# Two small reorderings in a fused attention and expert kernel: where the norm scales of every second group are made, and which of two PSUM copies goes first

## The chip, the cores and the metric

The kernel runs on one core of one Trainium2 chip. The metric is the device time of one execution in microseconds (us), as the median of several runs. The profiled execution is one more run with its own time.

## The reference: attention with normalised queries and keys, then eight experts with a limited capacity

Shapes: q, k, v are 8 batches x 12 heads x 448 rows x 64; the experts are 8, each with two weight matrices (768x1024 and 1024x768) and room for 80 rows.

```
rmsnorm(x, g) = x / sqrt(mean(x*x, -1) + 1e-6) * g
scores = rmsnorm(q) @ rmsnorm(k).T / 8
attn   = softmax(scores) @ v                # becomes x: 3584 rows of 768
logits = x @ w_gate ; expert = argmax(logits) ; gate = max softmax prob
each expert keeps its 80 rows of highest gate
out[rows] = gate * (relu(x[rows] @ w1[e]) @ w2[e])   # all other rows 0
```

## The kernel before: a hand-written order of slots

The 96 heads are handled four at a time, as 24 groups g (three per batch). A group has seven rounds. A round is one `score` (two 448-wide score products on TensorE, `ps`, L359, and their exponential on ScalarE, `at`, L362), one `presum` (VectorE adds `at` into the running sum `sm`, L392 and L394) and one `av` (TensorE, `po`, L376). The kernel is written out as a list of slots. Slot s issues the scores of rounds 2s and 2s+1 and the sums and products of the two rounds before. Group g begins in slot b0 = 7g//2. Every engine works through its own instructions in the order in which the slots issue them. Within a slot the order is: the slot's loads (`begins`), the two scores, `pre`, the presums, `mid`, the products `av`, then the lists `ahead` and `end`.

Preparation of a group is spread over the slots before it:

- `load_qk` in slot b0-11 (SyncE's queue; q and k have four buffers in all, so a load waits for `normalise` of the group two before).
- `square` (ScalarE, L270) and `squares` (VectorE row sums `ms`, L278) in slots b0-7 and b0-6.
- `rstd` in slot b0-5: two ScalarE instructions (Ln L289, Exp L290), then three short ones on VectorE (L291 to L293). `normalise` for q (a=0) follows in the same slot, for k (a=1) one slot later; both are VectorE, L306.
- `transp` for k and then for q in slot b0-2: 28 transposes on TensorE (`tp`, L314) and two ScalarE copies out of PSUM, `qkT` (L349 for k, L347 for q). These two are called the pair below. For odd g, slot b0-5 of group g is slot b0-2 of group g-1, so the pair of group g-1 stands in the `end` list of the slot whose `mid` list holds `rstd(g)`.

Around it run, per batch: `zl` (48 TensorE products for gate logits and softmax sums, L411, which need `sm` and `us` of the batch's three groups; slot b0+5 of its last group), `gate1` (ScalarE copies L421 and L423, a VectorE add L424), `gate1v`, `gate2` and others, and `merge`, which keeps a list of the best rows per expert. `merge` makes the row of gate weights (`row`: eight transposes, ScalarE copy L543, needed by the comparisons `vbeat`, L550 and L553). `xout` turns a group's result into rows (16 transposes into `xp`, ScalarE copy `xb`, L654) and stores it to HBM. For the first group of each batch but the first, `xout` falls into the same `end` list as `row` of the batch before.

PSUM buffers: the tag `sc` has two, shared in turn by every `ps`, by the k half of the pair, by `zl`, and by `merge`'s scratch, `row` included. The tag `tp` has one: the q half of the pair, `xp`, the turned gate sums. `at` has six buffers in SBUF.

In the code the lists are run so, at the end of each slot:

```
for f, a in ahead.pop(s, []) + end.pop(s, []):
    f(*a)
```

After the last group the experts run: gather of rows, two products per expert, scaling and a scatter of the output.

Of the kernel before, what the change touches and what calls it, by code (L numbers as in the profile page):

```python
# [21 lines left out]
def kernel(  # L22
# [31 lines left out]
    NQ = H // 4  # L54
# [178 lines left out]
    with av_stack:  # L233
# [3 lines left out]
        st = [dict() for _ in range(NG)]  # L237
# [74 lines left out]
        def turned(o, w, p):  # L312
            one = ident if w.dtype == F32 else identb
            nc.tensor.transpose(o, w, one[p, p], tile_position=(p.start, 0))  # L314
# [36 lines left out]
        def score(r):  # L351
            g, x = divmod(r, RD)
            T0, T1 = st[g]["T0"], st[g]["T1"]
            ps = scps.tile([128, 2, 512], F32, tag="sc", name="ps")
            at = apool.tile([128, 2, S], F32, tag="at", name="at")
            for u in range(2):
                for hh in range(2):
                    d = slice(hh * D, (hh + 1) * D)
                    nc.tensor.matmul(ps[u * 64:u * 64 + 64, hh, :S],  # L359
                                     T1[d, u, x * 64:(x + 1) * 64], T0[d, u, :],  # L360
                                     start=True, stop=True)
            nc.scalar.activation(at[:], ps[:, :, :S], AF.Exp)  # L362
            st[g]["at%d" % x] = at

        def av(r):
            g, x = divmod(r, RD)
            vt, at = st[g]["v"], st[g]["at%d" % x]
            if x == 0:
                po = pops.tile([128, 2, 512], F32, tag="po", name="po")
                other = po if g < NG - 1 else tpps.tile([128, 2, 512], F32, tag="tp", name="po")  # L370
                st[g]["po"] = (po, other)
            po = st[g]["po"]
            for u in range(2):
                p = slice(u * 64, u * 64 + 64)
                for hh in range(2):
                    nc.tensor.matmul(po[u][hh * D:(hh + 1) * D, u, :S],  # L376
                                     vt[p, hh * NX + x, :], at[p, hh, :],
                                     start=(x == 0), stop=(x == RD - 1))
            if x == RD - 1:
                st[g]["us"] = upool.tile([128, 2, S], F32, tag="us", name="us")  # L380

                n = 2 if g < NG - 1 else 1
                nc.scalar.copy(st[g]["us"][:, :n], po[0][:, :n, :S])  # L383
                if n < 2:
                    nc.vector.tensor_copy(st[g]["us"][:, n:], po[1][:, n:, :S])
# [253 lines left out]
        def xout(g):  # L639

            b, i = divmod(g, NQ)
            pool, tag = ((tpps, "tp"), (scps, "sc"), (pops, "po"))[
                max(0, g - NG + 3) or int(i == NQ - 1)]
            xp = pool.tile([128, 2, 512], F32, tag=tag, name="xp")
            us = st[g]["us"]
            for j in range(NJ + 1):
                for u in range(2):
                    c = slice((2 * j + u) * 64, (2 * j + u) * 64 + 64)
                    for hh in range(2):
                        p = slice(64 * hh, 64 * hh + 64)  # L650
                        t = min(j * 128, S - 128)
                        turned(xp[:, hh, c], us[p, u, t:t + 128], p)
            xb = prep.tile([128, NJ + 1, 256], F32, tag="xb", name="xb")
            nc.scalar.copy(xb[:].rearrange("p j (u hh d) -> p hh (j u) d", u=2, hh=2),  # L654
                           xp[:].rearrange("p hh (k d) -> p hh k d", d=D))
            st[g]["xb"] = xb
            if g < NG - 2:
                xstore(g)

        def xstore(g):  # L660
            b, i = divmod(g, NQ)
            xb = st[g]["xb"]
            rows = xr_dram[b * S:(b + 1) * S, i * 256:(i + 1) * 256].rearrange(
                "(p x) d -> p x d", x=NX)
            for t in range(2):
                nc.sync.dma_start(out=rows[:, t:SM // 64:2], in_=xb[64 * t:64 * t + 64, :NJ])
            nc.sync.dma_start(out=rows[:, NX - 1], in_=xb[64:, NJ])
# [25 lines left out]
        begins, pre, mid, end = {}, {}, {}, {}  # L693

        def at_slot(where, s, f, *a):
            where.setdefault(s, []).append((f, a))

        ahead = {}

        def first(s, f, *a):  # L700
            ahead.setdefault(s, []).append((f, a))
# [15 lines left out]
        for g in range(NG):  # L717
            b0 = g * RD // 2
            at_slot(begins, max(b0 - 11, -10), load_qk, g)
            at_slot(begins, b0 - 4, load_v, g)  # L720
            if g:
                for a in range(2):
                    at_slot(mid, b0 - 7 + a if g > 1 else -1, square, g, a)
                    at_slot(end, b0 - 7 + a if g > 1 else -1, squares, g, a)
                at_slot(mid, b0 - 5 if g > 1 else 0, rstd, g)
                for a in range(2):
                    at_slot(mid, b0 - 5 + a if g > 1 else 0, normalise, g, a)
            if g:
                for a in (0, 1) if g == 1 else (1, 0):
                    at_slot(end, b0 - 2 + (a if g == 1 else 0), transp, g, a)  # L730
            if g < NG - 2:
                i = g % NQ
                x0 = ((NQ * (g // NQ) - 1) * RD // 2 + 10 + 3 * i) if g >= NQ else 6 + 3 * i
                at_slot(end, b0 + 6 if i == NQ - 1 else x0, xout, g)
        for b in range(B):
            b0 = (NQ * b + NQ - 1) * RD // 2
            if b == B - 1:
                at_slot(end, b0 + 3, zl, b, range(NQ - 1))
                at_slot(end, b0 + 4, xout, NG - 2)
                at_slot(end, b0 + 4, zl, b, range(NQ - 1, NQ))  # L740
                at_slot(end, b0 + 4, gate1, b)
                at_slot(end, b0 + 4, xout, NG - 1)
                at_slot(end, b0 + 5, gate1t, b)
                at_slot(mid, b0 + 6, gate1v, b)
                continue
            first(b0 + 5, zl, b, range(NQ))
            first(b0 + 5, gate1, b)
            at_slot(end, b0 + 6, gate1t, b)
            at_slot(mid, b0 + 7, gate1v, b)
            at_slot(mid, b0 + 7, gate2, b)  # L750
            at_slot(mid, b0 + 8, gate2i, b)
            at_slot(end, b0 + 8, gate2x, b)
            at_slot(pre, b0 + 9, gate2b, b)
            at_slot(pre, b0 + 9, gate2p, b)
            for t, fs in enumerate(merge(b)):


                if b == B - 2 and t > 3:
                    at_slot(end, b0 + 12 + t, fs[0])
                    continue  # L760
                s = 15 + b % 2 if b < B - 2 else 13
                (first if t else lambda *a: at_slot(end, *a))(
                    b0 + (10, 10, 12, s, 18 + b % 2, 20 + b % 2)[t], fs[0])
                for n, f in enumerate(fs[1:]):
                    at_slot(end, b0 + (10, 11, 12, s)[t], f)
# [11 lines left out]
        for e in range(E):  # L777
            for i in range(2):
                s = 9 + 23 * (2 * e + i) // 5
# [11 lines left out]
        for s in range(-10, NS + 6):  # L791
            for f, a in begins.pop(s, []):
                f(*a)
            S2 = [r for r in (2 * s, 2 * s + 1) if 0 <= r < NG * RD]
            A2 = [r for r in (2 * s - 2, 2 * s - 1) if 0 <= r < NG * RD]

            for r in A2:
                if r % RD == RD - 1 and r < A2[-1]:
                    av(r)
            for r in S2:  # L800
                score(r)
            for f, a in pre.pop(s, []):
                f(*a)
            for r in A2:
                presum(r)
            for f, a in mid.pop(s, []):
                f(*a)
            for r in A2:
                if r % RD < RD - 1 or r == A2[-1]:
                    av(r)  # L810
            for f, a in ahead.pop(s, []) + end.pop(s, []):
                f(*a)
        assert not ahead
        assert not begins and not pre and not mid and not end
    mpool = ctx.enter_context(tc.tile_pool(name="moe_sb", bufs=2))

# [39 lines left out]
    ahead = tpool.tile([128, NT, CAP], BF16, tag="ahead", name="ahead")  # L856
# [187 lines left out]
```

## Time and profile before

| | |
|---|---|
| median of 3 runs | 422.82 us (422.19 to 422.96) |
| profiled execution | 423.0 us, its span 421.3 us |
| TensorE (PE) busy | 399.1 us, 95% |
| VectorE (DVE) busy | 357.5 us, 85% |
| ScalarE (ACT) busy | 314.9 us, 75% |
| GpSimd (POOL) busy | 73.5 us, 17% |
| granted TensorE clock, mean | 0.998 |

The span is from the first to the last instruction; 1.7 us of the execution's time lies around it. The ends of matmuls in the profile are modelled. "Idle before" in a row is the time in which the engine had nothing running before that instruction, with what ended it. A row of the timeline merges neighbouring instructions of a kind, with their count.

### The profile page before, as it was taken

What the parts mean: (1) busy time and instruction counts of PE and PEld (TensorE: products, weight loads), DVE (VectorE), ACT (ScalarE), POOL (GpSimd) and SP (SyncE); (2) the same over time, 40 slices, a digit from 0 to 9 for tenths busy, and PEclk for the clock granted to TensorE, in tenths of its full rate; (3) what the DMA queues carried; (4) which work ended last, traced back from release to release, by engine and by line L of the source; (5) the groups of instructions that cost most, each with busy time, mean ns of one, the idle gap of its engine ahead of it and who ended that gap; (6) DMA issues with size and microseconds to landing.
All of it is one profiled execution on the core that took longest, in us unless ns stands there. A gap on an engine that the chain in (4) does not pass through costs nothing.

```text
span 421.3 us, 12543 instructions
## 1 busy us (share of the span) xinstructions
PE 399.1 (95%) x5289; PEld 194.9 (46%) x5289; DVE 357.5 (85%) x641; ACT 314.9 (75%) x479; POOL 73.5 (17%) x118
## 2 busy tenths in 40 slices
PE   6799999999989999999899999999999999889993
PEld 6334444444444445444444444443444443448882
DVE  5699889998999999989999999989999779735550
ACT  5898979997889799979798799878997784202120
POOL 2000001301040205100420024001500050134321
PEclk9999999999999999999999999999999999999999
DMA  7355599999959999999799969999799298869981
GB/s 261 123 149 140 152 224 317 282 254 268 287 166 206 326 230 274 242 237 320 234 236 233 338 172 195 232 286 338 170 237 312 59 358 211 270 213 339 342 301 47
DMA packets 75983, 100.91 MB, mean 240 GB/s; under 512 B 8344, under 2 KB 65176, under 8 KB 75928
## 3 DMA queue, kind: packets, MB, share of 16 engines
q1 hardware_dynamic: 59856, 70.53, 52.2%
q0 software_dynamic: 15776, 29.13, 36.1%
q8 instruction: 41, 0.67, 0.6%
q10 hardware_dynamic: 296, 0.46, 0.4%
q14 instruction: 14, 0.11, 0.1%
HBM read 101.11 MB, written 39.89 MB: 335 GB/s over the span
## 4 chain that ended last, share of the span: by engine, by line
PE 69%; DMA 12%; DVE 10%; ACT 5%; issue 2%; SPq 0%; POOLq 0%; DVEq 0%; ACTq 0%
PE ps L359 26%; PE po L376 26%; DMA w_sb<-wb_scratch 5%; PE zl L411 4%; DMA qk<-in_k_dram 4%; PE tp L314 3%; PE xp L314 3%; DVE ms L278 2%; DVE sm L394 2%; DMA xr_scratch<-xb 2%; PE py L992 1%; DVE qn L306 1%; PE ph L973 1%; ACT qkT L349 1%; DMA xg<-xr_scratch,idxG 1%
## 5 line engine op out<-in xcount | busy, mean ns | idle before, releaser
L359 PE MATMUL ps<-qkT 64*64 64x448 f32 x1344 | 147.9, 548 | 7.6 <-ACT qkT L349 3.2
L362 ACT ACTIVATE at<-ps 128x896 f32<-128x896 f32 x168 | 146.4, 931 | 2.5 <-PE ps L359 1.6
L376 PE MATMUL po<-at,vt 64*64 64x448 f32 x1344 | 142.4, 537 | 0.1
L394 DVE TENSOR_TENSOR sm<-sm,at 128x896 f32<-128x896 f32 x120 | 132.0, 1100 | 2.9
L376 PEld LDWEIGHTS po<-at,vt 64*64 64x64 f32 x1344 | 50.0, 133 | 74.9 <-issue 64.3
L359 PEld LDWEIGHTS ps<-qkT 64*64 64x64 f32 x1344 | 43.1, 132 | 73.2 <-issue 23.5
L278 DVE TENSOR_REDUCE ms<-sq 128x14 f32<-128x896 f32 (+1 forms) x50 | 51.9, 1044 | 6.6 <-ACT sq L270 6.4
L306 DVE TENSOR_TENSOR qn<-qk,rs 128x896 f32<-128x896 f32 (+1 forms) x50 | 52.5, 1052 | 1.9
L270 ACT ACTIVATE sq<-qk 128x896 f32<-128x896 f32 (+1 forms) x50 | 46.3, 929 | 2.8 <-DMA qk<-in_q_dram 2.8
L518 POOL CAST pt<-gw 128x4 bf16<-128x4 f32 x8 | 6.9, 866 | 201.9 <-DVE gw L491 201.9
L977 ACT ACTIVATE h_sb<-ph 128x320 bf16<-128x320 f32 x16 | 7.0, 437 | 39.8 <-PE ph L973 39.8
L654 ACT COPY xb<-xp 128x1024 f32<-128x1024 f32 x24 | 24.3, 1011 | 9.7 <-PE xp L314 9.6
L314 PEld LDWEIGHTS tp<-ident,qn 64*128 64x128 f32 x672 | 23.4, 139 | 11.1 <-issue 5.3
L314 PE MATMUL tp<-ident,qn 64*128 64x64 f32 x672 | 26.9, 226 | 0.0
L383 ACT COPY us<-po 128x896 f32<-128x896 f32 (+1 forms) x24 | 21.4, 893 | 6.2 <-PE po L376 6.2
L392 DVE TENSOR_TENSOR sm<-at 128x896 f32<-128x896 f32 x24 | 25.9, 1081 | 0.0
L347 ACT ACTIVATE qkT<-tp,gqk 128x896 f32<-128x896 f32 x23 | 23.5, 1023 | 0.0
L349 ACT COPY qkT<-tp 128x896 f32<-128x896 f32 x24 | 21.9, 913 | 1.3 <-PE tp L314 1.2
L992 PE MATMUL py<-w_sb,h_sb 128*80 128x384 bf16 (+1 forms) x136 | 22.2, 317 | 0.6 <-DMA w_sb<-wb_scratch 0.6
L996 DVE TENSOR_SCALAR yo<-py,gwT 80x384 f32<-80x384 f32 (+1 forms) x16 | 9.5, 600 | 14.9 <-PE py L992 14.7
L411 PE MATMUL zl<-us,wgs 64*32 64x448 f32 x192 | 21.0, 540 | 0.0
L411 PE MATMUL zl<-sm,zsel 64*32 64x448 f32 x192 | 20.5, 540 | 0.0
(170 smaller groups left out, 412.0 us busy)
## 6 DMA issues: line engine op xcount, KB each, us to landing
wb_scratch<-in_moe_w_dram POOLq DMA_DIRECT2D x20, 768.0 KB, 14.9
w_sb<-wb_scratch SPq DMA_DIRECT2D x9, 1536.0 KB, 8.1
vt<-in_v_dram SPq DMA_DIRECT2D x24, 448.0 KB, 6.3
out_dram<-zeros SPq DMA_DIRECT2D x28, 384.0 KB, 8.2
qk<-in_q_dram SPq DMA_DIRECT2D x23, 448.0 KB, 5.0
qk<-in_k_dram SPq DMA_DIRECT2D x23, 448.0 KB, 6.6
xr_scratch<-xb SPq DMA_DIRECT2D x48, 192.0 KB, 10.2
w_sb<-in_moe_w_dram POOLq DMA_DIRECT2D x6, 1536.0 KB, 15.7
```

The source lines that it names most:

```text
L270: nc.scalar.activation(st[g]["sq%d" % a][:, lo:hi], st[g]["qk"][a][:, lo:hi], AF.Square)
L278: nc.vector.reduce_sum(out=st[g]["ms"][:, a, lo:hi], in_=st[g]["sq%d" % a][:, lo:hi], axis=AX.X)
L306: nc.vector.tensor_mul(qn[:].rearrange("p (x hh) d -> p hh x d", hh=2)[:, h0:h1], qk[:, lo:hi].rearrange("p (hh x) d -> p hh x d", x=NX), ...
L314: nc.tensor.transpose(o, w, one[p, p], tile_position=(p.start, 0))
L349: nc.scalar.copy(T[:], tp[:, :, :S])
L359: nc.tensor.matmul(ps[u * 64:u * 64 + 64, hh, :S], T1[d, u, x * 64:(x + 1) * 64], T0[d, u, :], start=True, stop=True)
L362: nc.scalar.activation(at[:], ps[:, :, :S], AF.Exp)
L376: nc.tensor.matmul(po[u][hh * D:(hh + 1) * D, u, :S], vt[p, hh * NX + x, :], at[p, hh, :], start=(x == 0), stop=(x == RD - 1))
L392: nc.vector.tensor_add(s["sm"][:], s["at0"][:], s["at1"][:])
L394: nc.vector.tensor_add(s["sm"][:], s["sm"][:], s["at%d" % x][:])
L411: nc.tensor.matmul(t[32 * c:32 * c + 32, r, :S], w, x, start=(i == 0), stop=(i == NQ - 1))
L992: nc.tensor.matmul(py[:, :c1 - c0], h_sb[:, fc, :], chunk(e, 1, fc)[:, c0:c1], start=(fc == 0), stop=(fc == FC - 1))
```

## The change: what is reordered

Two things are put elsewhere in the order; no instruction is added or taken away.

1. For odd g above 1 (g = 3, 5, ..., 23: 11 groups), `rstd(g)` and `normalise(g, 0)` go from the `mid` list of slot b0-5 to its `end` list, where they stand behind the pair of group g-1. `normalise(g, 1)` stays in `mid` of the next slot. What stands in `ahead` of that slot now comes before them too, and what the batch loop puts into `end` comes behind them, as before.
2. `xout` is split: for the first group of each batch but the first (g = 3, 6, ..., 21: 7 groups) its copy and store (`xcopy`) go into a new list `after`, run behind `end`. The copy of `row` then stands ahead of the copy of `xb`.

```diff
+            st[g]["xp"] = xp
+            if not (g % NQ == 0 and g >= NQ):
+                xcopy(g)
+
+        def xcopy(g):
+            xp = st[g]["xp"]
             xb = prep.tile([128, NJ + 1, 256], F32, tag="xb", name="xb")
             nc.scalar.copy(xb[:].rearrange("p j (u hh d) -> p hh (j u) d", u=2, hh=2),
                            xp[:].rearrange("p hh (k d) -> p hh k d", d=D))
...
-        ahead = {}
+        ahead, after = {}, {}
...
-                at_slot(mid, b0 - 5 if g > 1 else 0, rstd, g)
+                late = g > 1 and g % 2
+                at_slot(end if late else mid, b0 - 5 if g > 1 else 0, rstd, g)
                 for a in range(2):
-                    at_slot(mid, b0 - 5 + a if g > 1 else 0, normalise, g, a)
+                    at_slot(end if late and not a else mid, b0 - 5 + a if g > 1 else 0,
+                            normalise, g, a)
...
                 at_slot(end, b0 + 6 if i == NQ - 1 else x0, xout, g)
+                if i == 0 and g >= NQ:
+                    at_slot(after, x0, xcopy, g)
...
-            for f, a in ahead.pop(s, []) + end.pop(s, []):
+            for f, a in ahead.pop(s, []) + end.pop(s, []) + after.pop(s, []):
                 f(*a)
```

## Rows read from the trace of the kernel before

**Rows 1.** Busy time by stage: one period of two batches, 206.67 to 294.11 us

```profile
206.67:294.11 87.44, 85.90 (x1164) 38.02 (x1164) 83.04 (x139) 76.37 (x117) 15.26 (x24) 1.00 0.97 245
```

**Rows 2.** Timeline of PE: start, duration, what, count, idle before and its releaser

```profile
204.45 0.98 PE L359 MATMUL ps<-qkT 64*64 64x448 f32 x8
...
206.67 0.98 PE L359 MATMUL ps<-qkT 64*64 64x448 f32 x8 [1.23 <-ACT qkT L349]
...
210.21 0.98 PE L359 MATMUL ps<-qkT 64*64 64x448 f32 x8
211.63 0.98 PE L359 MATMUL ps<-qkT 64*64 64x448 f32 x8 [0.44 <-ACT row L543]
...
292.43 0.98 PE L359 MATMUL ps<-qkT 64*64 64x448 f32 x8
294.11 0.98 PE L359 MATMUL ps<-qkT 64*64 64x448 f32 x8 [0.69 <-ACT qkT L349]
```

**Rows 3.** Chain of waits: start, duration, what (a pair of scores without a wait)

```profile
214.12 1.50 PE ps L359 x16
```

**Rows 4.** Timeline of ACT around the stalls at 206.67 and 211.63

```profile
205.25 0.32 ACT L289 ACTIVATE rs<-ms,eps 128x28 f32<-128x28 f32 x1 [1.05 <-DVE ms L278]
205.59 0.23 ACT L290 ACTIVATE rs<-rs 128x28 f32<-128x28 f32 x1
205.73 0.89 ACT L349 COPY qkT<-tp 128x896 f32<-128x896 f32 x1
...
210.08 1.01 ACT L654 COPY xb<-xp 128x1024 f32<-128x1024 f32 x1
210.99 0.59 ACT L543 COPY row<-mp 128x512 f32<-128x512 f32 x1
```

**Rows 5.** Timeline of ACT, first instruction behind the pair in group 17's slot

```profile
237.08 1.75 ACT L362 ACTIVATE at<-ps 128x896 f32<-128x896 f32 x2
```

**Rows 6.** Timeline of DVE from group 17's norm scales to the next batch's gate sums

```profile
233.73 0.18 DVE L291 SCALAR_TENSOR_TENSOR nw<-rs 128x28 f32<-128x28 f32 x1
...
235.53 0.63 DVE L424 TENSOR_TENSOR zsb<-zsb,zo 128x448 f32<-128x448 f32 x1
236.07 0.19 DVE L603 TENSOR_TENSOR rnk<-back,eq 128x32 f32<-128x32 f32 x1
...
249.23 0.19 DVE L489 TENSOR_REDUCE lsum<-lex 128x4 f32<-128x32 f32 x1 [0.20 <-ACT lex L481]
...
270.58 2.28 DVE L394 TENSOR_TENSOR sm<-sm,at 128x896 f32<-128x896 f32 x2
...
276.56 0.63 DVE L424 TENSOR_TENSOR zsb<-zsb,zo 128x448 f32<-128x448 f32 x1 [1.70 <-ACT zo L423]
```

**Rows 7.** Timeline of PE: a gate product of the batch's third group

```profile
274.51 0.54 PE L411 MATMUL zl<-sm,zsel 64*32 64x448 f32 x2
```

**Rows 8.** Timelines of DVE and ACT around group 16's norm scales

```profile
219.71 1.08 DVE L278 TENSOR_REDUCE ms<-sq 128x14 f32<-128x896 f32 x1
...
221.17 0.38 ACT L289 ACTIVATE rs<-ms,eps 128x28 f32<-128x28 f32 x1
...
222.12 1.01 ACT L654 COPY xb<-xp 128x1024 f32<-128x1024 f32 x1 [0.31 <-PE xp L314]
...
226.07 0.91 ACT L383 COPY us<-po 128x896 f32<-128x896 f32 x1 [0.45 <-PE po L376]
```

**Rows 9.** Timeline of DVE in the first period and after the last norm scales

```profile
72.51 1.09 DVE L278 TENSOR_REDUCE ms<-sq 128x14 f32<-128x896 f32 x1 [0.56 <-ACT sq L270]
74.40 0.19 DVE L489 TENSOR_REDUCE lsum<-lex 128x4 f32<-128x32 f32 x1 [0.81 <-ACT lex L481]
...
336.67 0.19 DVE L489 TENSOR_REDUCE lsum<-lex 128x4 f32<-128x32 f32 x1 [2.19 <-ACT lex L481]
```

**Rows 10.** Timeline of ACT: squares that wait for a load of q

```profile
196.54 0.95 ACT L270 ACTIVATE sq<-qk 128x896 f32<-128x896 f32 x1 [0.29 <-DMA qk<-in_q_dram]
...
284.67 0.96 ACT L270 ACTIVATE sq<-qk 128x896 f32<-128x896 f32 x1 [0.98 <-DMA qk<-in_q_dram]
```

More of the change, by code (lines that the diff above doesn't have):

```diff
@@ L810 @@
                     av(r)
-            for f, a in ahead.pop(s, []) + end.pop(s, []):
+            for f, a in ahead.pop(s, []) + end.pop(s, []) + after.pop(s, []):
                 f(*a)
-        assert not ahead
+        assert not ahead and not after
         assert not begins and not pre and not mid and not end
```

## Prediction

> **What bounds the kernel now.** I read the busy times by stage first. The attention part repeats itself every two batches (six groups), and in one such period TensorE is busy 85.90 of 87.44 us and VectorE 83.04 [rows 1]. So there are two full engines, not one, and the reader should keep the second in mind: whatever TensorE gains, VectorE must keep up with.
>
> Next I went through TensorE's timeline for idle time. In a period it has two places only. In one, the second score of a slot waits for the copy `qkT` of k (L349), because that copy holds one of the two `sc` buffers. In the other it waits for the copy of `row` (L543), for the same reason [rows 2]. Each occurs three times in the run: groups 9, 15 and 21 for the first (1.24, 1.23 and 0.69 us idle, the first not shown), and the three later slots of `row` for the second (0.44 us each). ScalarE's timeline tells why. Ahead of the `qkT` copy stand Ln and Exp of the next group's norm scales, and Ln waits 1.05 us for a VectorE row sum; ahead of `row` stands the `xb` copy of 1.01 us [rows 4]. These are the very two things that the change puts behind.
>
> Last I followed VectorE. Between 233.73 and 276.56 it stands idle twice: 0.20 us, and 1.70 us before the add of the gate sums [rows 6]. Its gaps otherwise are those between one instruction and the next. It has about 1.9 us in a period to give.
>
> **What the change removes.** Two scores without a wait take 1.50 us, 0.75 each [rows 3]. With the stall, the second begins 206.67 - 204.45 = 2.22 us after the first, so 1.47 us too late; group 9 looks the same. Group 21: 294.11 - 292.43 = 1.68, so 0.93. The `row` place: 211.63 - 210.21 = 1.42, so 0.67, three times [rows 2]. Is the full amount won? The pair's k copy could start when ScalarE falls idle, 205.25 - 1.05 = 204.20, takes 0.89 and so ends at 205.09, before the score's unstalled time 204.45 + 0.75 = 205.20. The `row` copy starts up to 0.91 us earlier (210.99 - 210.08); it waits at most for its own transposes, and needs to end only 0.67 earlier [rows 4]. So yes for both: 2 x 1.47 + 0.93 + 3 x 0.67 = 5.88 us. The lower bound is nothing, if another release ends as late.
>
> The profile's idle column would give less: 2 x 1.23 + 0.69 + 3 x 0.44 = 4.47 us [rows 2]. The Trainium skill (Perfetto Trace Analysis, section Tensor Engine Instruction) says that the end of a matmul in a profile is estimated from its size, not observed. By that the idle time after an end is too uncertain to be summed, and starts are the better measure; with the column the sum below would come out 1.4 us later.
>
> **What the change adds: a wait of VectorE.** At groups 3, 9, 15 and 21 the moved Ln and Exp cost VectorE nothing: it runs late there, and reaches L291 well after Exp. At groups 7, 13 and 19 I price them at nothing too: Exp comes later by the pair's two copies, and VectorE is still busy with its presums then. At groups 5, 11, 17 and 23 the slot also holds `zl` and `gate1`, and Ln now has to wait for all of them and for the pair. For group 17: the pair ends so that ScalarE's next instruction starts at 237.08 [rows 5]; from Ln's start to Exp's end are 205.59 + 0.23 - 205.25 = 0.57 us [rows 4]; L291 can start at about 237.68 instead of 233.73 [rows 6], 3.95 us later. The add L424 now comes before it, which takes back 236.07 - 235.53 = 0.54 [rows 6]. What is queued behind it on VectorE, all presums and the next normalisations, is about 3.4 us late against TensorE.
>
> Who waits for that? The nearest hard need is the next batch's `zl`, whose third group needs the last presum. That presum ends at 270.58 + 2.28 = 272.86 [rows 6], and TensorE takes it at 274.51 [rows 7]: 1.65 us of slack. On the way VectorE can save only the 0.20 us of idle time [rows 6]. So TensorE comes 3.4 - 0.2 - 1.65 = 1.6 us later there. Some of it may appear earlier in the half period, as a wait of ScalarE for the row sums of group 18, but the total is the same. After `zl` the lag is gone in VectorE's 1.70 us of idle time [rows 6].
>
> Group 11 is the same within 0.2: 1.5. Group 5 comes in the first period, where VectorE has 0.56 and 0.81 us of idle time [rows 9]: 3.4 - 1.4 - 1.6 = 0.4, say 0.5. Group 23 is followed by no more row sums and normalisations, and VectorE idles 2.19 us [rows 9] and about as much again: 0. Sum 3.6 us. Below, the bound is nothing, if some slack is larger than it looks; above, the full lags of 3.4 us at three places, 10 us. I take the slack from the nearest rows as it stands.
>
> **A smaller one.** In the other half period TensorE's gain of 1.47 + 0.67 = 2.1 us makes VectorE late by that much. Group 16's Ln then waits: its row sum ends at 219.71 + 1.08 = 220.79 and Ln starts at 221.17, slack 0.38 [rows 8], so 1.7 us of wait. ScalarE has 0.31 and 0.45 us of idle time behind it [rows 8] to make up for it. Left are 0 to 1.0 us; I take half, 0.5, also for group 10, and 0.2 for group 22, where the lag is smaller. Sum 1.2.
>
> **Loads.** SyncE's loads of q wait for `normalise` of the group two before, so a late VectorE issues them late. Two squares wait for such a load now, 0.29 and 0.98 us [rows 10]. If they land when the queue comes to them, nothing changes; if they land later by VectorE's lag of some 1.5 us, each may cost that. I put 0.2 us. The stores of `xb` go out about 0.6 us later (the `row` copy, [rows 4]); nothing waits for them before the experts' gather. Nothing changes in the experts' part.
>
> **Sum.** -5.88 + 3.6 + 1.2 + 0.2 = -0.9 us. The profiled execution took 423.0 us, so 422.1; the median of the runs is 0.2 lower: 421.9 us, 0.2% less than before. A change of 0.2%, 0.85 us, is about what a measurement of this kernel can tell from none, so the forecast stands on that edge.
>
> A cross-check by VectorE alone: its idle time per period goes from 1.9 us to the new wait at L291, 237.68 - (233.73 + 0.54) = 3.4 less the lag of about 1.6 that it has by then, some 1.8. The period therefore hardly shrinks, and what is won comes from the ends: the first half period, where VectorE has idle time, and the last, after which it has less work.
>
> **Rivals.**
> - *VectorE's lag is absorbed.* If `at` buffers and the normalised tiles hold enough slack (the transposes need them some 4 us after they are made), the 3.6 and 1.2 us are not paid, or only half of them. Half gives -5.88 + 2.4 + 0.2 = -3.3: 419.5; nothing paid gives 417. For it: TensorE's rows show no other wait of that size. Against it: VectorE has 1.9 us in 87 to catch up [rows 1, 6], and `zl` needs its last presum within 1.65. Chance 0.18.
> - *Late loads make it slower.* The load of q for groups 15 and 21 is issued behind a VectorE that is 1.5 to 2 us late, and ScalarE then holds back the copy of `po` that TensorE needs next. Two such waits of 1.5 us give -0.9 - 0.2 + 3.0 = +1.9: 424.7. It decides from about 0.9 us each on. For it: ScalarE waits for both loads already [rows 10]. Against it: those loads stand behind others on SyncE's queue, so that the issue need not be what sets the landing. Chance 0.20.
> - *Gain and payback cancel.* The stalls go, but the lag is paid in full a little earlier, at group 18's row sums and the first period alike, or TensorE wins only the idle column. -0.9 + 0.9 = 0: 422.8. Chance 0.17.
>
> **How the numbers follow.** The forecast has 0.45. Its own range is 420.9 to 422.8, from the unknowns of 1.2 us around its sum. It lies above the 0.2% limit by a hair: 0.27 of it count as faster, 0.18 as same. The first rival adds 0.18 to faster. The second gives 0.18 to slower and 0.02 to same, the third 0.15 to same and 0.02 to slower. Together: faster 0.45, same 0.35, slower 0.20. The range that should hold 8 in 10 reaches half way into the first rival and the second: 419.3 to 424.2.
>
> **What the changed profile would show.** Right: no idle time of TensorE before a second score with `qkT` or `row` as releaser; in groups 5, 11 and 17, VectorE idle for 1 to 2 us before L291, released by Exp L290, and no idle time before the add of the next batch; a stretch between the two `zl` after them that is 1.5 us longer, and the stretches with groups 9 and 15 about 1.6 us shorter. Wrong: if the stretch after group 17's `zl` keeps its length, the lag was absorbed and the time is near 419. If ScalarE's waits for loads of q grow past 2 us, the second rival holds. If TensorE still waits for `qkT` L349, the first step was wrong.

## The result, and the profile after

The changed kernel took 426.81 us (median of 4 runs, 424.95 to 428.65) against 422.50 (4 runs, 422.18 to 422.96) on the same chip: ratio 1.010, interval 1.005 to 1.015. It is slower by about 1%, where 0.2% faster was forecast; the time lies outside the range. The profiled execution took 426.27 us, its span 424.6. Part of the difference is not the change's: in the profiled execution the granted TensorE clock was low in the first 20 us, before any moved instruction, and the stretch with it is 1.08 us longer. The kernel before has executions of that kind too (last section). The one execution of the changed kernel with a mean clock as high as 0.996 took 424.95 us, so some 2.5 us are left without it.

A table by stretch tells more than the totals. The marks are the starts of the first `zl` product (L411) of each batch on TensorE's timeline. The first column is the length in the kernel before, the others are differences from it. "To 0" is the start, "5 to 6" the stretch from batch 5's to batch 6's first product, and "the end" is that of TensorE's last product. Each column is the one profiled execution of its kernel. The other kernels are the runs of the next section: "mod 3" has late norm scales for groups 3, 9, 15 and 21 alone, "mod 5" for 5, 11, 17 and 23 alone, and in "paced" kernels the copies of the experts' weights are held to their slots.

| stretch | before | after | copies only | scales mod 3 | scales mod 5 | after, two weight copies earlier | after, paced | mod 3, paced, old copies |
|---|---|---|---|---|---|---|---|---|
| to 0 | 57.66 | +1.08 | +0.59 | +0.82 | +1.16 | +0.51 | +0.04 | -0.03 |
| 0 to 1 | 40.44 | +0.39 | +0.22 | +0.23 | +1.50 | +0.38 | +0.39 | 0.00 |
| 1 to 2 | 46.40 | -1.24 | -0.25 | -1.24 | -0.01 | -1.22 | -1.24 | -1.14 |
| 2 to 3 | 41.03 | +1.50 | +0.25 | +0.78 | +2.71 | +1.51 | +1.51 | +0.66 |
| 3 to 4 | 46.40 | -0.28 | -0.24 | -1.33 | -0.01 | -1.35 | -1.11 | -1.13 |
| 4 to 5 | 41.03 | +1.50 | +0.25 | +0.59 | +2.71 | +1.65 | +1.64 | +0.79 |
| 5 to 6 | 46.41 | +0.85 | -0.26 | +4.63 | +4.87 | -1.37 | -1.37 | -1.14 |
| 6 to 7 | 33.32 | +0.31 | +0.24 | +0.25 | +0.08 | +0.31 | +0.31 | +0.01 |
| 7 to the end | 61.87 | -0.85 | +0.77 | -0.86 | -0.68 | -0.80 | -1.27 | -1.36 |

In the column "after", 0 to 1, 2 to 3 and 4 to 5 came near the forecast in size (+0.5, +1.5, +1.6). Stretch 1 to 2, forecast 1.6 shorter, is 1.24 shorter. Stretches 3 to 4 and 5 to 6, forecast shorter by 1.6 and about 1.4, are 0.28 shorter and 0.85 longer. The last stretch is shorter in nearly every kernel here, so it was probably long by chance in the profile of before.

First the signs that came true. TensorE's timeline after, at the place of [rows 2]:

```profile
207.24 1.73 PE L359 MATMUL ps<-qkT 64*64 64x448 f32 x16
...
210.86 0.33 PE L314 MATMUL mp<-identb,eqb 64*72 64x64 bf16 x8 [0.23 <-ACT at L362]
```

Both scores of the slot run as one row of 16 products; the 1.23 us are gone. A small new wait stands behind them. ScalarE's timeline answers to [rows 4]:

```profile
206.92 0.91 ACT L349 COPY qkT<-tp 128x896 f32<-128x896 f32 x1 [1.02 <-PE tp L314]
207.72 1.01 ACT L347 ACTIVATE qkT<-tp,gqk 128x896 f32<-128x896 f32 x1
208.62 0.32 ACT L289 ACTIVATE rs<-ms,eps 128x28 f32<-128x28 f32 x1
```

Ln now stands behind the pair and waits for nothing. VectorE's timeline, at the place of [rows 6]:

```profile
236.97 0.63 DVE L424 TENSOR_TENSOR zsb<-zsb,zo 128x448 f32<-128x448 f32 x1 [1.47 <-ACT zo L423]
239.15 0.19 DVE L291 SCALAR_TENSOR_TENSOR nw<-rs 128x28 f32<-128x28 f32 x1 [1.55 <-ACT rs L290]
...
279.50 0.62 DVE L424 TENSOR_TENSOR zsb<-zsb,zo 128x448 f32<-128x448 f32 x1
```

VectorE now idles 1.47 + 1.55 us at group 17, and no longer before the next batch's L424: the lag of about 3 us lasts until there, as forecast. Groups 5, 11 and 23 show the same 1.55.

Where TensorE pays for it was forecast less well. The next `zl` waits for nothing. The payment comes earlier in the stretch, on ScalarE and then on TensorE:

```profile
253.86 0.32 ACT L289 ACTIVATE rs<-ms,eps 128x28 f32<-128x28 f32 x1 [1.05 <-DVE ms L278]
```
```profile
256.10 0.33 PE L314 MATMUL mp<-identb,eqb 64*72 64x64 bf16 x8 [0.58 <-ACT at L362]
```

Ln of group 18 waits for a late row sum, the exponential `at` behind it is late, and the transposes of `merge` wait for that. TensorE's next transposes (`gw`) start 257.08 - 233.38 = 23.70 us behind batch 4's first `zl` product, where they started 254.48 - 231.93 = 22.55 us behind it before: 1.15 of the 1.50 us are lost by then. Group 12 shows the same.

Now what did not come as forecast. ScalarE's timeline answers to [rows 10], TensorE's shows who waits in turn:

```profile
199.48 0.95 ACT L270 ACTIVATE sq<-qk 128x896 f32<-128x896 f32 x1 [1.49 <-DMA qk<-in_q_dram]
...
289.28 0.95 ACT L270 ACTIVATE sq<-qk 128x896 f32<-128x896 f32 x1 [2.65 <-DMA qk<-in_q_dram]
290.14 0.89 ACT L383 COPY us<-po 128x896 f32<-128x896 f32 x1
```
```profile
201.28 0.98 PE L376 MATMUL po<-at,vt 64*64 64x448 f32 x8 [0.62 <-ACT us L383]
...
291.08 0.98 PE L376 MATMUL po<-at,vt 64*64 64x448 f32 x8 [1.77 <-ACT us L383]
```

The squares of groups 15 and 21 wait 1.49 and 2.65 us for q (0.29 and 0.98 before), the copy of `po` stands behind them, and TensorE loses 0.62 and 1.77 us. Why q lands late is seen on two queues. SyncE's, after:

```profile
265.96 5.47 SPq L242 DMA_DIRECT2D vt<-in_v_dram  x1
271.53 0.42 SPq L242 DMA_DIRECT2D qk<-in_q_dram  x1
```

The load is issued at 271.53 and its square can start at 289.28: 17.75 us for 448 KB, where the median of the q loads in this profile is 5.6. GpSimd's timeline, before and then after (`L204` issues a copy of weights from HBM to HBM):

```profile
249.69 0.96 POOL L518 CAST pt<-gw 128x4 bf16<-128x4 f32 x1 [36.37 <-DVE gw L491]
...
253.75 3.03 POOL L204 DMA_DIRECT2D wb_scratch<-in_moe_w_dram  x4
...
257.25 0.82 POOL L204 DMA_DIRECT2D wb_scratch<-in_moe_w_dram  x1
```
```profile
254.19 0.97 POOL L518 CAST pt<-gw 128x4 bf16<-128x4 f32 x1 [39.17 <-DVE gw L491]
...
258.25 3.03 POOL L204 DMA_DIRECT2D wb_scratch<-in_moe_w_dram  x4
...
261.76 0.82 POOL L204 DMA_DIRECT2D wb_scratch<-in_moe_w_dram  x1
```

GpSimd waits for the gate weights `gw` of batch 4. Behind that wait stand five weight copies of 768 KB (L204), which all go out at once. Measured from batch 4's first `zl` product, `gw` came 249.69 - 231.93 = 17.76 us later before, and 254.19 - 233.38 = 20.81 after: the lag of VectorE. q for group 21 landed 284.67 - 253.75 = 30.9 us after the first copy before, and 289.28 - 258.25 = 31.0 after. The trace fits the rival as well: from q's own issue to its landing are 284.67 - 266.85 = 17.82 us before and 17.75 after. So the suspicion to test: what sets the landing is when the five copies are through, not when q is issued.

While the five copies run, the 16 DMA engines are busy all the time and yet move less; then the rate goes up (after; the last three numbers of a row are the granted clock, the DMA share, which can add up to more than 1, and GB/s):

```profile
270.00:275.00 5.00, 5.00 (x56) 1.74 (x48) 4.90 (x6) 5.00 (x7) 0.00 (x0) 1.00 1.12 229
285.00:290.00 5.00, 4.31 (x48) 1.53 (x40) 4.86 (x9) 2.35 (x4) 0.00 (x0) 1.00 1.06 374
```

By the packets of GpSimd's queue in the trace, the last one ends 28.3 us after the first copy's issue, and q lands 2.8 us later. In all six profiles with five copies there (before, after, the copies alone and the three thirds below), q of group 21 lands 2.0 to 2.8 us and q of group 15 0.2 to 0.6 us behind that packet; the time from q's issue to its landing varies more, for group 21 from 17.8 to 19.8 us.

### The profile page after: what moved, and what is told of

It reads as the page before. It is cut to its first block, busy times and chain, and to the rows that moved or that the text cites. A ratio compares the mean times of both kernels' runs of the same rounds, so it can differ in the third digit from the quotient of the medians.

```text
span 424.6 us, 12538 instructions
## 1 busy us (share of the span) xinstructions
PE 403.0 (95%) x5289; PEld 193.6 (46%) x5289; DVE 357.4 (84%) x641; ACT 315.6 (74%) x479; POOL 74.6 (18%) x118
## 4 chain that ended last, share of the span: by engine, by line
PE 65%; DVE 16%; ACT 8%; DMA 6%; issue 3%; POOLq 0%; DVEq 0%; ACTq 0%
PE ps L359 22%; PE po L376 21%; DMA qk<-in_q_dram 5%; PE zl L411 4%; DVE sm L394 4%; PE py L1002 4%; PE ph L983 3%; PE tp L314 3%; DVE ms L278 3%; ACT at L362 3%; DVE qn L306 3%; PE xp L314 2%; ACT us L383 1%; ACT qkT L349 1%; DVE sm L392 1%
## 5 line engine op out<-in xcount | busy, mean ns | idle before, releaser
L359 PE MATMUL ps<-qkT 64*64 64x448 f32 x1344 | 149.6, 558 | 1.9 <-DVE qkT L344 0.9
L411 PE MATMUL zl<-us,wgs 64*32 64x448 f32 x192 | 21.1, 541 | 0.0
L411 PE MATMUL zl<-sm,zsel 64*32 64x448 f32 x192 | 20.6, 541 | 0.0
L314 PEld LDWEIGHTS xp<-ident,us 64*128 64x128 f32 x384 | 14.1, 139 | 12.0 <-ACT at L362 10.6
```

Of the source, the lines that this page charges most:

```text
L359: nc.tensor.matmul(ps[u * 64:u * 64 + 64, hh, :S], T1[d, u, x * 64:(x + 1) * 64], T0[d, u, :], start=True, stop=True)
L411: nc.tensor.matmul(t[32 * c:32 * c + 32, r, :S], w, x, start=(i == 0), stop=(i == NQ - 1))
```

## The experiments

Each was timed beside the kernel before on the same chip, whose medians there were 423.63, 423.90 and 422.87 us in the three groups of runs. Lines of code are those of the changed kernel. A ratio is that of the record with its 95% interval, and not the quotient of the medians beside it.

**The copies alone** (the new place of `xcopy`, without the late scales; for all its seven groups, though the expectation names the three with a stall).

```diff
-                late = g > 1 and g % 2
+                late = False
```

> Only the second part of the change: the norm scales stay where the kernel before has them, and only the copy of the x rows of groups 6, 12 and 18 is put behind the copy of the gate weights' row. Theory A (this part does what the diff says, and PE's idle time of 0.67 us behind each of three row copies is a gain): 2.0 us less than before, about 420.5 us. Theory B (the gain is taken back at the next wait of ACT or of the x-row transfers): 422.5 us, within 0.5. In both, PE's idle behind the row copy is gone.

Measured: 423.86 us, ratio 1.001 (0.999 to 1.003). Theory B. TensorE's idle time behind `row` went, but ScalarE's copy of `po` comes later by the order, and the next product waits:

```profile
123.68 0.58 ACT L543 COPY row<-mp 128x512 f32<-128x512 f32 x1 [0.18 <-PE mp L314]
124.16 1.02 ACT L660 COPY xb<-xp 128x1024 f32<-128x1024 f32 x1
125.07 1.75 ACT L362 ACTIVATE at<-ps 128x896 f32<-128x896 f32 x2
126.67 0.97 ACT L270 ACTIVATE sq<-qk 128x896 f32<-128x896 f32 x1
127.51 0.93 ACT L383 COPY us<-po 128x896 f32<-128x896 f32 x1
```
```profile
128.49 0.98 PE L376 MATMUL po<-at,vt 64*64 64x448 f32 x8 [0.18 <-ACT us L383]
```

The table has 0.25 us won in each stretch with the stall and 0.22 to 0.25 lost in each without one. 2.0 us had been expected, and nothing came.

**The late scales, in thirds.** For groups 3, 9, 15 and 21 with the new copy order; for 5, 11, 17 and 23 with the old one; for 7, 13 and 19 with the old one.

```diff
-                late = g > 1 and g % 2
+                late = g % 6 == 3
```

(in the others `g % 6 == 5`, and `g > 1 and g % 6 == 1`).

> The copy order of the change, and the late norm scales for groups 3, 9, 15 and 21 alone. It keeps the removal of the stalls of 1.47, 1.47 and 0.93 us and leaves out every group with a wait of VectorE in the trace after (5, 11, 17) and the groups 7, 13 and 19, whose late normalise holds back the q loads of groups 9, 15 and 21. Theory A (the stalls removed are gains, and what was lost came from the other groups): 3.9 + 2.0 = 5.9 us less than before, about 416.6 us. Theory B (the removed stalls come back as other waits, whatever the other groups do): about 420.5 us, the copies' part alone, or 422.5.

> The late norm scales for groups 5, 11, 17 and 23 alone, and the copies as before. Theory A (VectorE's wait behind the batch's sums puts some 3.4 us of lag on it, and this is paid at PE in the amounts 0.5, 1.5 and 1.6): about 3.6 us more than before, 426.1 us, with the waits of SquareE's squares on the q loads of groups 15 and 21 near 0.3 and 1.0 us as before. Theory B (the lag is absorbed, and the loss after is the late q loads alone): 422.5 us, within 0.5.

> The late norm scales for groups 7, 13 and 19 alone, and the copies as before. These are the groups whose normalise frees the buffers of the q loads of groups 9, 15 and 21. Theory A (the late loads come from these groups' own new place): ACT's squares of groups 15 and 21 wait about 1.5 and 2.6 us for q where they waited 0.29 and 0.98, PE then waits 0.6 and 1.8 us for ACT's copies, and the time is about 424.9 us. Theory B (the loads are late only because VectorE lags from groups 5, 11 and 17): the waits stay at 0.3 and 1.0, and the time at 422.5 us, within 0.5.

Measured: 422.23 us, ratio 0.999 (0.996 to 1.002); 430.58 us, ratio 1.017 (1.014 to 1.020); 423.67 us, ratio 1.000 (0.998 to 1.002).

The first shows the gain (1.24 and 1.33 us) in two of three stretches, and its profiled execution loses it all in the third, where ScalarE waits 3.50 us for q:

```profile
287.04 0.95 ACT L270 ACTIVATE sq<-qk 128x896 f32<-128x896 f32 x1 [3.50 <-DMA qk<-in_q_dram]
```

Group 19, whose normalise frees the buffer of this load, was not moved. So my Theory A of that run was wrong about the price of the other groups: they are not needed for a late q. That execution, of 426.86 us, is one of three out of 12 above 426; seven took 421.4 to 422.4, so most seem to be spared this loss, but none of them has a trace. The second falls on the far side of its Theory A: the lag costs 1.50, 2.71 and 2.71 us, not 0.5, 1.5 and 1.6, and the q wait of group 21 is 3.94 us, not 1. (The profiled execution, 435.32 us, is the longest of seven. The median is 6.95 us above that of the kernel before, and 1.50 + 2.71 + 2.71 = 6.92: the late q of the profile seems not to be in most executions.) Its timelines of TensorE and of ScalarE show where the additional 1.2 us goes:

```profile
89.98 1.79 PE L359 MATMUL ps<-qkT 64*64 64x448 f32 x16 [1.39 <-ACT own L574]
```
```profile
89.04 0.32 ACT L289 ACTIVATE rs<-ms,eps 128x28 f32<-128x28 f32 x1 [1.67 <-DVE ms L278]
89.39 0.23 ACT L290 ACTIVATE rs<-rs 128x28 f32<-128x28 f32 x1
89.52 0.41 ACT L574 COPY own<-mp 128x320 f32<-128x320 f32 x1
```

The late VectorE makes group 7's Ln wait in its old place, and the copy `own` behind it holds a score up; groups 13 and 19 show the same. The paced kernels with groups 3, 9, 15 and 21 alone (below) have that stall too, of 0.4 to 0.7 us. In the full change these Ln are moved, and the stall is not there: the third of groups 7, 13 and 19, which I had priced at nothing, takes a stall from the other two. (The two others together, without it, were not run.) The third run has q waits of 0.56 and 1.74 us, between its theories, and no difference in time: no stretch between the first and the last `zl` differs from the kernel before by more than 0.02. The loads are somewhat later than before, but so is the last packet of the five copies, by its distance from the first issue (29.5 us for group 21, 28.1 before).

**More buffers for q and k.**

```diff
-        qkpool = qk_stack.enter_context(tc.tile_pool(name="qk", bufs=4, side="right"))
+        qkpool = qk_stack.enter_context(tc.tile_pool(name="qk", bufs=5, side="right"))
...
-                st[g]["sq%d" % a] = qkpool.tile([128, NB, D], F32, tag="sq", name="sq", bufs=2)
+                st[g]["sq%d" % a] = qkpool.tile([128, NB, D], F32, tag="sq", name="sq", bufs=1)
```

> The changed kernel with five buffers for q and k instead of four, and one for the squares instead of two (the same memory). The load of q no longer needs the buffer that the normalise of two groups earlier frees. Theory A (the loads of groups 15 and 21 are late because they wait for a late normalise): ACT's waits for them, 1.49 and 2.65 us after the change, fall under 0.3, PE's 0.62 and 1.77 behind ACT's copies go, and the kernel is 2.4 us faster than the changed one, some 2 us over the kernel before. Theory B (the loads are issued behind a backlog of their queue and land when the five weight copies that GpSimd issues in one go behind the gate weights are through the DMA engines): the two waits stay within 0.5 us of what they were, and so does the time, some 3 to 4 us over the kernel before.

Measured: ratio 1.059 (1.056 to 1.063), 448.65 us in the profiled execution. It tells nothing about the loads: the fifth buffer was paid with one of the squares', and squares waited 32.5 us in all for VectorE's row sums. The experiment changed two things, and the second drowned the first.

**Two weight copies earlier**, in the changed kernel, in the kernel of groups 3, 9, 15 and 21, and in the kernel before.

```diff
-                    at_slot(begins, s + 2 * half, stage_w, e, i, half)
+                    t = s + 2 * half
+                    at_slot(begins, t - (t in (38, 59)), stage_w, e, i, half)
```

> The changed kernel with two of its weight copies (those of slots 38 and 59) put one slot earlier, so that GpSimd issues them ahead of its wait for the gate weights of batches 2 and 4: four copies go out in one go behind each of these waits, where there were five. Theory B (these copies fill the DMA engines for some 31 us, and the q load of groups 15 and 21 lands when they are through): the stretch ends a fifth, some 6 us, sooner, ACT's waits of 1.49 and 2.65 us vanish, and the kernel is 2.4 us faster than the changed one, about 2 us over the kernel before. Theory A (the q loads are late because they are issued behind a late normalise): they still wait, 1 us or more, and the time stays within 0.7 us of the changed kernel's.

> The late norm scales for groups 3, 9, 15 and 21 alone, the copy order of the change, and the same two weight copies one slot earlier. Theory B (PE's stalls removed in the odd batches are real gains of 1.2 to 1.3 us each, and what took them back in the run without the earlier weight copies was the wait of 3.50 us for the q load of group 21 with the fall of the granted clock behind it): no such wait, no fall, and 2 to 3 us less than the kernel before. Theory C (the gains are taken back elsewhere): within 0.7 us of the kernel before.

> The control: the kernel before with the same two weight copies one slot earlier. Its waits for the q loads of groups 15 and 21 were 0.29 and 0.98 us and held no matmul up, so both theories expect them to vanish and the time to stay within 0.5 us of the kernel before.

Measured: 423.78 us, ratio 1.002 (1.000 to 1.005); 422.89 us, 0.999 (0.996 to 1.001); 424.07 us, 1.000 (0.999 to 1.002). The changed kernel lost its 1% with nothing done to the scales, the order of ScalarE's copies or the loads; it came out even with the kernel before, 2 us better than Theory B had it. SyncE's queue and ScalarE's timeline of that run:

```profile
270.74 0.42 SPq L242 DMA_DIRECT2D qk<-in_q_dram  x1
```
```profile
285.02 0.97 ACT L270 ACTIVATE sq<-qk 128x896 f32<-128x896 f32 x1
```

q of group 21 is issued 3.70 us ahead of batch 5's first product (274.44), against 4.38 in the changed kernel: later, and yet the square doesn't wait. Stretches 3 to 4 and 5 to 6 are 1.07 and 2.22 us shorter than in the changed kernel. So the issue behind a late normalise is not the cause. But five copies now go out behind batch 3 instead, and there a new wait appears in the profiles of all three kernels, the kernel before included:

```profile
245.05 0.95 ACT L270 ACTIVATE sq<-qk 128x896 f32<-128x896 f32 x1 [2.19 <-DMA qk<-in_q_dram]
```
```profile
246.85 1.36 PE L376 MATMUL po<-at,vt 64*64 64x448 f32 x12 [2.06 <-ACT us L383]
```

These are of the kernel before with the two copies moved (group 18). The wait goes where the five go; stretch 4 to 5 is 2.30 us longer with it. (The control's profiled execution took 424.66 us at a mean clock of 0.997, but others took 422.30 at 0.995 and 422.65 at 0.994, and its median is that of the kernel before: this wait is not in every execution.) The expectation of 2 to 3 us won in the second kernel fell: its waits moved to two other loads, one behind these five (1.91 us), one behind the four of batch 2 (1.31 us), so four in one go can be too many as well.

**Weight copies held to their slots.** GpSimd reads one element of a recent `at` ahead of each copy, so that it can't run ahead of the other engines; nothing of the computation changes.

```diff
+        pace = cpool.tile([1, 1], F32, name="pace")
+
+        def paced(s, *a):
+            g, x = divmod(2 * s - 1, RD)
+            nc.gpsimd.tensor_copy(pace[:, :], st[g]["at%d" % x][:1, 0, :1])
+            stage_w(*a)
...
-                    at_slot(begins, s + 2 * half, stage_w, e, i, half)
+                    at_slot(begins, s + 2 * half, paced, s + 2 * half, e, i, half)
```

> The late norm scales for groups 3, 9, 15 and 21 alone and the copy order of the change; ahead of each weight copy GpSimd reads one element of the scores' exponentials of the slot before, so that the copies go out one by one at their slots and not four or five in one go. Theory B (copies in one go fill the DMA engines, and the q loads behind them are late): no square waits for a q load in batches 2 to 6 and no matmul for one, the intervals between the batches' sums are those of the runs so far without their q waits (+0.2, -1.2, +0.8, -1.3, +0.6, -1.4, +0.2, and -0.9 behind the last), 3.0 us less than the kernel before in all, some 420.8 us. Theory C (the q loads are late for their own place in SyncE's queue): waits of 1 us or more stay at groups 15 or 21, and the time is within 0.7 us of the kernel before.

> The changed kernel with its weight copies held to their slots in the same way. Theory B: the waits of 1.49 and 2.65 us for q vanish, the waits of VectorE behind the sums of batches 0, 2, 4 and 6 stay (+0.4, +1.5, +1.5), the stalls removed in the odd batches count in full (-1.2, -1.35, -1.4), with -0.5 at the end: some 1 us less than the kernel before. Theory C: 3 us or more over the kernel before, as the change was.

> The control: the kernel before with its weight copies held to their slots. No late load held a matmul up in it, so both theories expect its time within 0.5 us of the kernel before; if the pacing itself costs or gives something, it shows here.

> The late norm scales for groups 3, 9, 15 and 21 alone, the copies in the order of the kernel before, the weight copies held to their slots. The copy order alone was worth 0.25 us less in each odd batch and 0.25 more in each even one. Theory A (the copies are worth nothing in all): within 0.4 us of the run with the copy order of the change, some 2.8 us less than the kernel before. Theory B (the copy order is needed for the gain, since the late scales and the copies share ACT): 1 us or more slower than that run.

Measured, against 422.87 us: 421.59, ratio 0.996 (0.994 to 0.998); 422.87, ratio 1.000 (0.999 to 1.002); 422.51, ratio 0.999 (0.997 to 1.002); 420.20, ratio 0.994 (0.992 to 0.996). GpSimd's timeline of the last:

```profile
254.03 0.82 POOL L204 DMA_DIRECT2D wb_scratch<-in_moe_w_dram  x1
257.13 0.26 POOL L713 COPY pace<-at 1x1 f32<-1x1 f32 x1 [2.28 <-ACT at L362]
257.57 0.74 POOL L204 DMA_DIRECT2D wb_scratch<-in_moe_w_dram  x1 [0.17 <-issue]
268.03 0.17 POOL L713 COPY pace<-at 1x1 f32<-1x1 f32 x1 [9.73 <-ACT at L362]
268.27 0.73 POOL L204 DMA_DIRECT2D wb_scratch<-in_moe_w_dram  x1
```

One copy at a time, and in none of the four kernels does a square wait for q after the start of the run. Theory B holds stretch by stretch: the first has +0.24, -1.24, +0.79, -1.11, +0.78, -1.38 and +0.24 from batch 0 to 7. The changed kernel, the second, keeps its VectorE waits and its gains, and they cancel. The square of group 21 in it, which had waited 2.65 us:

```profile
284.78 0.97 ACT L270 ACTIVATE sq<-qk 128x896 f32<-128x896 f32 x1
```

Theory B had some 1 us less than the kernel before there; the times are even. The pacing alone (the third) is worth nothing that can be told from zero. Of the 3.0 us expected of the first kernel 1.3 came by the medians; the 0.9 at the end are not its own, since the control has them too. The kernel with the old copy order has the best time of all, 0.6% less than the kernel before; its interval overlaps that of the first. Theory B of that run fell; Theory A expected it within 0.4 us of the first, and by stretches from batch 0 to 7 it is (-1.95 against -1.68), while the medians lie 1.4 apart; the rest is in the start (+1.16 in the first's profile) and the end.

## Why the prediction was wrong, step by step

Two steps failed: the loads, priced at 0.2 us, and the `row` part of the gain, priced at 2.0.

- *Loads*: this is the larger. I wrote "I put 0.2 us". Against the paced changed kernel, stretches 3 to 4 and 5 to 6 are 0.83 and 2.22 us longer in the changed one: 3.05 us.
- *What the change removes*: right in kind, too large in size. I put 5.88 us. TensorE's stalls behind `qkT` and `row` went, but stretches 1 to 2, 3 to 4 and 5 to 6 of the paced changed kernel, where no load disturbs, gave 1.24, 1.11 and 1.37: 3.7 us. The `row` part is what missed. With the copies alone, 0.75 us came in these three stretches and 0.96 went in the four others: nothing in all. It was moved to the next wait, for the copy of `po`. My check asked whether the k copy and `row` would end in time, not what ScalarE does late afterwards. The `qkT` part held: the late scales of groups 3, 9, 15 and 21 without the copies, paced, gave 1.14 + 1.13 + 1.14 = 3.4 us in these stretches, where I had 3.87 less the 1.2 of *A smaller one*.
- *The wait of VectorE*: right in kind, near in size partly by luck. I put 0.5 + 1.5 + 1.6 = 3.6; stretches 0 to 1, 2 to 3 and 4 to 5 gave 0.39 + 1.50 + 1.50 = 3.4. But 0.72 us of these stand in the run of the copies alone, so that about 2.7 are left for the norm scales (an estimate, as if the parts added up). They do not add up well: without any of the groups 5, 11 and 17 the first paced kernel already loses 0.24 + 0.79 + 0.78 there, and with them alone the loss is 6.9. The place was not `zl`, as I put first, but the row sums of group 18, which I had named as possible. Group 23, put at 0, is 0.31 longer, of which 0.24 are the copies'.
- *A smaller one*, 1.2 us at the even groups: the waits of Ln are there, 1.04, 1.17 and 0.76 us at groups 10, 16 and 22 of the paced changed kernel, and what they cost is inside the 3.7 above. The first and third step together forecast a gain of 5.88 - 1.2 = 4.7. So the sum of the three steps, -1.1, was off by 1.2 us: the paced changed kernel has 0.39 - 1.24 + 1.51 - 1.11 + 1.64 - 1.37 + 0.31 = +0.13 between the first and the last product, and a ratio of 1.000. That is the rival *Gain and payback cancel* in its number, once the loads are out of the way.
- The rival *Late loads make it slower* named the two loads, the wait of ScalarE and that of TensorE; its sign, a wait for q past 2 us, came (2.65), and its 424.7 was the nearest. Its 3.0 us for two equal waits met the 3.05 of two unequal ones. But it blamed the issue of the loads behind a late normalise, and the runs showed another cause. The sentence I held against it (the issue need not set the landing) was true, and I did not ask what sets it instead.
- A slip without consequence: 1.2 us around 421.9 is 420.7 to 423.1, not 420.9 to 422.8.

The cause, as far as the runs show it: GpSimd works in program order: in the changed kernel it waited 39.17 us for `gw` and issued no copy in that time. Its first instruction for a batch's list needs `gw` from VectorE, and every weight copy of the next ten slots stands behind that wait, four or five of them. VectorE's lag at groups 11 and 17 falls exactly on the batches (2 and 4) with five. The copies start 3 us later against TensorE and are through some 28 us after the first is issued (the 31 us of the expectations run to the landing of q), and the q load in their midst lands later by as much. The Trainium skill (DMA: Bandwidth & Descriptors, section Issuing engines are not separate DMA queues) says that transfers started by different engines run on the same 16 DMA engines and interleave; the 17.75 us for a load with a median of 5.6 agree.

What stays open: why q of group 21 took 19.84 us (267.20 to 287.04) in the profile of groups 3, 9, 15 and 21, where the copies began only 0.2 us later than before. The trace shows one step more: the last packet of the five copies ended 31.1 us after the first issue (28.1 before), and q landed 2.0 us behind it, as elsewhere. What made the copies 3 us slower there, and why most executions of that kernel seem to be spared it, is not shown.

## What to carry to other kernels

An instruction that waits holds back all that its queue has behind it, DMAs too: when a change makes an engine late, ask of every queue that waits for it what goes out in one go when the wait ends, and who reads data at that time. A wait for a load that is small before a change can mean that the stretch is near its bound by transfers, and that time won on the engines can end there. Pacing such transfers by a cheap read gave nothing by itself, but it took the 1% from the changed kernel. With it the late scales of groups 3, 9, 15 and 21 were 0.4% and 0.6% faster than the kernel before, with the new and the old copy order; without it the first of these could not be told from the kernel before (0.999, 0.996 to 1.002), though the medians lie as far apart (1.4 us, and 1.3 paced), and the second was not run. A stall's price is only what is left when the next wait has been looked for: 2.0 us behind `row` were worth nothing. And a profile is one execution: set its time beside those of the others before summing its stretches.

## What was not expected of the hardware

The granted clock differs between executions at the start, whose code is the same in all these kernels. In the changed kernel's profiled execution (windows: length, busy time and count of TensorE, its weight loads, VectorE, ScalarE and GpSimd, granted clock, DMA share, GB/s):

```profile
5.00:10.00 5.00, 2.82 (x28) 2.42 (x26) 4.86 (x13) 3.37 (x9) 0.00 (x0) 1.00 0.96 336
10.00:15.00 5.00, 3.59 (x32) 1.69 (x32) 2.58 (x6) 3.81 (x6) 0.00 (x0) 0.63 0.56 190
15.00:20.00 5.00, 5.00 (x38) 1.52 (x36) 3.58 (x7) 4.60 (x8) 0.00 (x0) 0.68 0.03 4
```

The full clock is 2.4 GHz and the other level 1.2; 0.63 and 0.68 are means of stretches with both. TensorE had idled 2.29 us before the product at 10.47 (1.76 in the kernel before, whose clock stayed at 1.00). That the one made the other was not tested. Among 29 executions of the kernel before on one chip, the 15 with a mean clock of 0.987 or 0.988 took 423.5 to 424.4 us, and of the 9 with 0.995 to 0.998 seven took 421.9 to 422.2: some 1.9 us, more than many edits are worth.

The clock can fall late in the run too. In the run with groups 3, 9, 15 and 21 TensorE idled 2.62 us before 288.83, waiting for ScalarE behind the late q:

```profile
280.00:290.00 10.00, 7.38 (x84) 2.62 (x80) 9.63 (x21) 6.26 (x9) 0.00 (x0) 0.96 1.03 315
290.00:300.00 10.00, 10.00 (x100) 4.54 (x100) 5.08 (x9) 6.30 (x12) 6.24 (x11) 0.70 0.95 257
```

Its stretch 5 to 6 is 6.0 us longer than with the weight copies paced (+4.63 against -1.38): more than twice the idle time. With 3.06 us of idle time in the run with groups 5, 11, 17 and 23 it fell to 0.76; behind 1.77 us in the changed kernel it stayed at 1.00.
